# One attention kernel on one core: output bank and read banks take turns by head, new plan with 203 VectorE tiles

## The chip, the core and the metric

The kernel runs on one core of a Trainium2 chip. Five engines work side by side, each on its own queue of instructions in a fixed order: TensorE (PE in the profile, its weight loads PEld), VectorE (DVE), ScalarE (ACT), GpSimd (POOL) and SyncE (SP, which here only issues DMAs). They meet through semaphores: an instruction that has to wait holds up everything behind it on its own engine. TensorE writes its results into PSUM, which has 128 partitions and eight banks; a bank holds 512 float32 numbers for each partition. The metric is the time of one execution on the device in microseconds (us), lower is better. The median of runs is compared.

## The reference

```python
B, H, S, D = 1, 32, 2048, 640
Dh = D // H                       # 20
def reference(q, k, v, t):
    eps = 1e-6
    qn = q / (jnp.sqrt((q * q).sum(axis=-1, keepdims=True)) + eps)
    kn = k / (jnp.sqrt((k * k).sum(axis=-1, keepdims=True)) + eps)
    logits = jnp.einsum('bhqd,bhkd->bhqk', qn, kn) * t[None, :, None, None]
    attn = _softmax(logits, axis=-1)
    return jnp.einsum('bhqk,bhkd->bhqd', attn, v)
```

There are 32 heads of 2048 queries and 2048 keys with 20 features each, all in bfloat16. The logits are bounded (normalized rows times t), so no maximum is subtracted; the sum of the exponentials comes out of a column of ones beside v.

## The kernel before

**Tiles.** The keys of a head lie in 16 blocks of 128 (R = 16), its queries in 4 quarters of 512 (NG = 4). One block of keys against one quarter of queries is a unit: 128 x 512 logits, one PSUM bank. Four units that go into the same output matmuls are a tile, so a head has 16 tiles and the kernel 512. A tile is either ScalarE's or VectorE's. `DVE_TILES` (L715) gives VectorE's number for each head, 5 to 8; they sum to 206, so 306 tiles (1224 units) are ScalarE's.

**ScalarE's path.** TensorE multiplies units into `psA` (five banks, used as a set of two and a set of three; `add_wave`, L1142, matmul at L1073, tasks `q3A`). ScalarE takes the exponential of a whole set at once from `psA` into `p_ring` (L1165, tasks `exp`), so sets of 1024 and 1536 columns alternate. An `exp` can start when its set is multiplied, and the set can be multiplied again when its `exp` is done.

**VectorE's path.** TensorE multiplies two units' worth of packed logits at a time into the two banks of `psD` (L1078, tasks `q2D`, "the pair"). VectorE reads both banks in one instruction into `xt` (L1216, tasks `t1`): this builds bit patterns of an approximate exponential. Three shifted copies of it (tasks `s0`, `s1`, `s2`) are made by GpSimd (L1246, `ss`) or VectorE (L1236 into `ss`, L1234 into `sp`); the four versions are weighted and summed by the output matmuls. `xt` has 8 slots, `ss` and `sp` 4. The next pair waits for the `t1` that reads the same banks (`bank_t1`).

**Output.** Each group of four output matmuls (L1094, tasks `pv`) multiplies one version of a tile with v and adds into one bank, `psO`. A ScalarE tile has one group, a VectorE tile four. When all groups of head h are in, VectorE transposes the bank into `oT` (L1107, task `tr`, in `add_fin`, L1103), and later divides and stores, for two heads together (L1116, L1124). The first output matmul of head h+1 overwrites the bank, so `pv_base` (L1100) makes every `pv` of head h+1 wait for `tr` of head h.

**Other work.** VectorE also squares, sums and normalizes q and k of heads to come (L923 to L969); SyncE loads, transposes and rotates them. Groups of four matmuls with a zero weight (`pvnil`, L1004 to L1010) are put into idle stretches of TensorE and add zero to the open output bank.

**Order.** No queue is written out by hand. `list_schedule` (L151) plays the whole kernel through with a duration for each task and lets each engine take, whenever it is free, the best ready task by some twenty rules. The numbers in these rules (`KNOBS`, L103) are chosen anew for each 10 us of planned time; the choices are packed into the integers of `STAGES` (L108). The durations are constants in the code: a group on TensorE takes `PE_MM` = 0.223 us (L712), a change of its kind of matmul 0.097 us (L412, L581). The order found is emitted, with semaphore waits worked out by `plan_waits` (L626). The planned times themselves do not reach the chip, only the order of each queue.

PSUM before: `psA` five banks, `psD` two, `psO` one.

Of the kernel before, what the change touches and what calls it, by code (L numbers as in the profile page):

```python
# [54 lines left out]
class Task:  # L55
    __slots__ = ("eng", "fn", "dur", "deps", "pri", "name", "lat", "dma", "n", "users",
                 "start", "end", "seq", "inc", "cnt", "rows", "work", "modes", "win", "trig",
                 "alt", "parts", "parent", "rem", "glue", "room", "next", "head", "wide", "slow", "sdur", "pair", "base", "two", "need")

    def __init__(self, eng, name, fn, dur, deps, pri, lat=0.0, dma=None):  # L60
        self.eng, self.name, self.fn, self.dur = eng, name, fn, dur
        self.deps = [d for d in deps if d is not None]
        self.pri, self.lat, self.dma = pri, lat, dma
        self.inc, self.cnt = False, 0
        self.rows, self.work, self.modes = 128, 512.0, None
        self.win, self.trig = 0.0, None
        self.alt, self.parts, self.parent, self.rem = None, [], None, 0
        self.glue, self.room, self.next, self.head, self.wide = [], 0.0, None, None, None


        self.slow, self.sdur, self.pair, self.base, self.two = False, 0.0, None, dur, None

        self.need = None


Wake = Task("DVE", "wake", None, 0.0, [], 0.0)


class Program:
# [27 lines left out]
        "WAITH": (0.3, 0.1, 0.6), "BLOG": (5, 3, 4, 7, 9, 99), "PTWO": (1, 0), "STAY": (1, 0), "URGE": (3, 2, 4, 6), "BOOST": (1.0, 0.0, 0.4, 4.0), "DPV": (0.0, 0.3, 0.65, 1.0)}  # L107
    STAGES = (121198495550, 386731570679, 77123854022, 617480453033, 541694991365, 26516008980, 28188130953, 628587374903, 9557073731, 415555843896, 209498320437, 646470623202, 136583393724, 671941958076, 672324246996, 792421957682, 689380213680, 803027612629, 379997812126, 638643698950, 639121345246, 531136220444, 376259042864, 376617779119, 221897598895, 374543095684, 221362179218, 787313552789, 415913386058, 208446558798, 427204335065, 465723747116, 401404110210, 428458674786, 432937268058, 619977817991, 207993392811, 516782334303, 568560126277, 529856924852, 435260979089, 428752721390, 619855720106, 632747624100, 787539313032, 787849807561, 633115376521, 774950211778, 788266765840, 736861074358, 722791283681, 515990522269, 287562967953, 747408491084, 537279315194, 325670581757, 376196432267)  # L108

    def __init__(self):  # L110
        self.tasks = []
        self.nsw = 0
        self.filler, self.fillers = None, []
# [6 lines left out]
    def schedule(self):  # L120
        self.list_schedule()
        for f in self.tasks:
            if f.parts:
# [27 lines left out]
    def list_schedule(self, until=None):  # L151
        self.stage = None
        for t in self.tasks:
            t.users = []
            t.trig = None
            if t.modes:
                self.use(t, 0)
            if t.alt:
                t.eng, t.parts, t.slow, t.dur = "DVE", [], False, t.base
        for i, t in enumerate(self.tasks):  # L160
            t.seq = i
            deps = []
            for d in t.deps:
                deps += d() if callable(d) else [d]
            t.deps = list(dict.fromkeys(deps))
            t.n = len(t.deps)
            for d in t.deps:
                d.users.append(t)
# [223 lines left out]
        base, at_ = [0.0], {"e": 0, "t": 0}  # L392
        left = collections.Counter(t.head for t in self.tasks if t.head is not None)
# [3 lines left out]
        def fill(now):  # L397
# [10 lines left out]
            t = self.filler()  # L408
# [3 lines left out]
            if last_pe[0] != "pv":  # L412
                t.end += max(0.0, 0.097 - (now - free["PE"]))
# [8 lines left out]
        while events or ready["POOL"]:  # L422
# [20 lines left out]
            for e in touched:  # L443
# [7 lines left out]
                if e in soon:  # L451
                    wide = e == "PE" and self.QHOLD and any(
                        now < w <= now + self.QHOLD and self.tasks[q].name[2] == "A" for q, w in soon["PE"].items())
                    held = [r for r in ready[e] if wide and r[2].name[0] == "q" and r[2].name[2] == "D" or r[2].name[:2] not in ("t1", "tr") and
# [23 lines left out]
                elif e == "DVE" and self.CONT:  # L478
# [21 lines left out]
                    elif not sh:  # L500
                        x = min(ready[e])
                    else:
# [5 lines left out]
                        continue  # L508
                    ready[e].remove(x)
# [68 lines left out]
                if e == "PE":  # L578
                    kind = "pv" if t.rows > 128 else t.name[:2]
                    if kind != last_pe[0]:  # L580
                        t.end += max(0.0, 0.097 - (now - free["PE"]))  # L581
                        self.nsw += 1
# [3 lines left out]
                    recent.append((t.end, t.work))  # L586
                    if t.head is not None:
# [4 lines left out]
                if t.name[:3] in ("exp", "t1."):  # L592
                    at_[t.name[0]] += 1
                done += 1
# [25 lines left out]
            if self.CONT:  # L620
                done += cont_fill(now)
        self.order, self.free, self.ready = order, free, ready
# [59 lines left out]
def bass_standalone__qk_norm__prompt_kernel(  # L682
# [42 lines left out]
    with ExitStack() as es:  # L725
# [34 lines left out]
        psD = es.enter_context(nc.psum_tensor("psD", [128, 1024], F32))  # L760
        psO = es.enter_context(nc.psum_tensor("psO", [128, 512], F32))
# [237 lines left out]
        for i in range(NWARM):  # L999
            warm.append(add("PE", "warm", lambda e, tk: e.matmul(psO[:, :], ones[:, 0:128], ones[:, :], start=True, stop=True), PE_MM,  # L1000
# [3 lines left out]
        def null_mm(eng):  # L1004
            last = None
            for g in range(NG):
                last = eng.matmul(psO[32 * g:32 * g + 32, :], nil[:, :], ones[:, :], start=False, stop=False,  # L1007
                                  skip_group_check=True, tile_position=(0, 32 * g))
            return last
        prog.filler = lambda: Task("PE", "pvnil", lambda e, tk: null_mm(e), PE_MM, [z_nil, z_one], 0.0)  # L1010

        def first_head(rinv):
# [28 lines left out]
            for i in range(NWARM2):  # L1041
                warm.append(add("PE", "warm", lambda e, tk: e.matmul(psO[:, :], ones[:, 0:128], ones[:, :], start=True, stop=True), PE_MM, [tk_], -198))
# [46 lines left out]
        def pv_mm(eng, h, w_of, rhs_of):  # L1089
# [3 lines left out]
            for g in range(NG):  # L1093
                last = eng.matmul(psO[32 * g:32 * g + 32, :], w_of(g), rhs_of(g), start=start,  # L1094
# [4 lines left out]

        def pv_base(h):  # L1100
            return [ld_v[h]] + z_v[h % NV] + ([lambda: [trO[h - 1]]] if h else warm)

        def add_fin(h):  # L1103
# [4 lines left out]
                oT_all[:, so, :, :].rearrange("p r d -> p (r d)"), psO[:, :]), 0.63,  # L1108
# [33 lines left out]
        def add_wave(w):  # L1142
# [12 lines left out]
            qk = add("PE", f"q3A{w}", lambda e, tk: f_qk(e), PE_MM + 0.01, deps, w - 10000.0)  # L1155
# [37 lines left out]
        def add_dgroup(jg):  # L1193
# [9 lines left out]
            for bs in ((0,), (1,)) if SPLIT[j % len(SPLIT)] else ((0, 1),):  # L1203
                def f_qk(eng, bs=bs):
                    last = None
                    for b in bs:
                        last = qk_pair(eng, h, c, dl, b, psD[:, 512 * b:512 * b + 512])
# [7 lines left out]
                def read(name, dst, o, add_, deps, pri):  # L1215
                    return add("DVE", name, lambda e, tk: e.tensor_scalar(  # L1216
                        dst[:, o + 2 * w0:o + 2 * (w0 + n)].bitcast(I32), psD[:, w0:w0 + n], W_MUL, add_, ALU.mult, ALU.add),
# [132 lines left out]
```

## Time and profile before

| what | number |
|---|---|
| time, median of 3 runs | 577.32 us (576.85 to 577.65) |
| the profiled execution, its own time | 577.27 us |
| its span, first to last instruction | 575.5 us |
| granted TensorE clock, mean | 0.999 |
| busy PE, PEld | 554.6, 160.7 us |
| busy DVE, ACT, POOL | 556.9, 558.6, 453.0 us |
| transposes of the output bank (L1107) | 32, 715 ns each, 22.9 us together |
| reads of the pair (L1216) | 206, 1216 ns each, 250.4 us together |
| shifts by POOL (L1246) | 356, 443.8 us together |
| shifts by VectorE into sp (L1234), into ss (L1236) | 155, 188.7 us; 17, 11.1 us |
| zero groups (L1007) | 68 matmuls, 5.7 us |
| HBM traffic | 18 GB/s over the span |

In the lists of the profile a row names the line, the engine, the operation and `out<-in` by the program's names, then the count; busy time counts time in which at least one such instruction ran, so overlapping instructions (ScalarE's, TensorE's) have a mean that times the count exceeds it. "Idle before" is time the engine stood still just before such an instruction, and "<-" names what ended it. In a timeline a row is start, length, engine, line, and in brackets the idle time before it. The profiled execution lies 0.05 us from the median, and 1.8 us of its time lie outside of its span.

### The profile page before, as it was taken

The numbers are of one execution on the slowest core, as the hardware profiler recorded it, in microseconds if no ns is written. First come the engines' busy times: TensorE is split into PE (matmuls) and PEld (weight loads), VectorE is DVE, ScalarE is ACT, GpSimd is POOL, SyncE is SP. The second block draws the span as 40 slices with busy tenths as digits, with TensorE's granted clock in tenths as the row PEclk, the third lists the DMA queues.
The fourth block names the chain that finished last, engine by engine and source line by source line (L and its number), as shares of the span: only waits on it lengthen the run. The fifth ranks groups of instructions, "written<-read, shape, count | busy, mean of one in ns | idle before, by whom it ended". The sixth has DMA issues, their size and how long they took to land.

```text
span 575.5 us, 14801 instructions
## 1 busy us (share of the span) xinstructions
PE 554.6 (96%) x6255; PEld 160.7 (28%) x6255; DVE 556.9 (97%) x661; ACT 558.6 (97%) x497; POOL 453.0 (79%) x406
## 2 busy tenths in 40 slices
PE   7999999999999999999999999999999999999997
PEld 2222232222222222222222232222222222223333
DVE  8999999999999999999999999999999999999997
ACT  6999999999999999999999999999999999999992
POOL 6586985898598985997768795887949888688972
PEclk9999999999999999999999999999999999999999
DMA  5544513553354403653046420563205540241000
GB/s 67 65 75 84 61 16 70 88 90 31 67 85 52 76 1 72 88 64 57 2 95 75 76 35 11 100 79 69 22 21 101 72 75 2 50 80 40 2 2 18
DMA packets 190770, 32.18 MB, mean 56 GB/s; under 512 B 170608, under 2 KB 190704, under 8 KB 190704
## 3 DMA queue, kind: packets, MB, share of 16 engines
q1 hardware_dynamic: 190560, 31.15, 35.3%
q8 instruction: 49, 0.80, 0.6%
q14 instruction: 17, 0.14, 0.1%
q10 hardware_dynamic: 144, 0.08, 0.1%
HBM read 7.87 MB, written 2.62 MB: 18 GB/s over the span
## 4 chain that ended last, share of the span: by engine, by line
ACT 86%; PE 10%; POOL 1%; DVE 1%; issue 0%; POOLq 0%
ACT p_ring L1165 86%; PE psO L1094 7%; PE psA L1073 2%; PE psD L1078 1%; DVE oT L1107 0%; POOL p_ring L1053 0%; DVE ss L1236 0%; POOL pcol L829 0%; POOL vph L770 0%; DVE xt L1216 0%; POOL vaug L770 0%; DVE rs_sum L926 0%; POOL pcol L823 0%; PE psO L1007 0%; DVE o_stage L1124 0%
## 5 line engine op out<-in xcount | busy, mean ns | idle before, releaser
L1165 ACT ACTIVATE p_ring<-psA 128x1024 bf16<-128x1024 f32 x490 | 555.1, 1369 | 2.5 <-PE psA L1073 2.2
L1246 POOL INT64_ADD ss<-xt x356 | 443.8, 1265 | 114.5 <-PE psO L1094 40.9
L1216 DVE TENSOR_SCALAR xt<-psD 128x1024 int32<-128x1024 f32 x206 | 250.4, 1216 | 5.5 <-PE psD L1078 4.7
L1234 DVE TENSOR_SCALAR sp<-xt 128x1040 int32<-128x1040 int32 x155 | 188.7, 1225 | 0.5 <-PE psO L1094 0.3
L1073 PE MATMUL psA<-qkT,kR 32*128 32x512 bf16 x968 | 164.5, 384 | 8.9 <-ACT p_ring L1165 7.3
L1094 PE MATMUL psO<-ss,vph 128*32 128x512 bf16 (+1 forms) x1852 | 166.2, 393 | 0.8 <-DVE oT L1107 0.7
L1094 PE MATMUL psO<-p_ring,vaug 128*32 128x512 bf16 x1224 | 112.1, 383 | 0.4 <-DVE oT L1107 0.4
L1073 PEld LDWEIGHTS psA<-qkT,kR 32*128 32x128 bf16 x968 | 40.0, 91 | 154.3 <-ACT p_ring L1165 146.8
L1094 PE MATMUL psO<-xt,vaug 128*32 128x512 bf16 (+1 forms) x824 | 82.2, 394 | 0.6 <-DVE oT L1107 0.3
L1094 PE MATMUL psO<-sp,vph 128*32 128x512 bf16 (+1 forms) x620 | 65.1, 408 | 0.0
L1094 PEld LDWEIGHTS psO<-ss,vph 128*32 128x32 f16 x1852 | 43.8, 94 | 58.9 <-issue 34.0
L1078 PE MATMUL psD<-qP,kR 64*128 64x512 bf16 x284 | 55.4, 387 | 1.7 <-DVE xt L1216 1.5
L1073 PE MATMUL psA<-qkT 32*128 32x512 bf16 x256 | 53.6, 384 | 1.7 <-ACT p_ring L1165 1.3
L1094 PEld LDWEIGHTS psO<-p_ring,vaug 128*32 128x32 bf16 x1224 | 29.8, 94 | 40.0 <-issue 29.4
L1094 PEld LDWEIGHTS psO<-xt,vaug 128*32 128x32 bf16 x824 | 21.7, 94 | 28.8 <-issue 18.6
L1107 DVE STREAM_TRANSPOSE oT<-psO 128x512 f32<-128x512 f32 x32 | 22.9, 715 | 6.9 <-PE psO L1094 6.4
L1078 PE MATMUL psD<-qP,qkT 64*128 64x512 bf16 x128 | 24.9, 386 | 0.8 <-DVE qP L979 0.6
L1078 PEld LDWEIGHTS psD<-qP,kR 64*128 64x128 bf16 x284 | 13.6, 92 | 39.2 <-issue 22.8
L1073 PEld LDWEIGHTS psA<-qkT 32*128 32x128 bf16 x256 | 12.9, 90 | 40.8 <-ACT p_ring L1165 38.4
L926 DVE TENSOR_REDUCE rs_sum<-sq 128x64 f32<-128x1280 bf16 (+1 forms) x17 | 23.1, 1357 | 0.0
L969 DVE TENSOR_TENSOR qkn<-qk_sb,rs_r 128x1280 bf16<-128x1280 bf16 (+1 forms) x17 | 22.9, 1367 | 0.0
L1094 PEld LDWEIGHTS psO<-sp,vph 128*32 128x32 f16 x620 | 16.3, 94 | 21.2 <-issue 10.4
(66 smaller groups left out, 129.1 us busy)
## 6 DMA issues: line engine op xcount, KB each, us to landing
kR<-qkT SPq DMA_DIRECT2D x62, 96.0 KB, 2.2
kR<-qkT SPq DMA_DIRECT2D x62, 64.0 KB, 2.1
qk_sb<-in_k_dram SPq DMA_DIRECT2D x32, 80.0 KB, 3.1
vaug<-in_v_dram SPq DMA_DIRECT2D x32, 80.0 KB, 3.3
qk_sb<-in_q_dram SPq DMA_DIRECT2D x124, 20.0 KB, 2.5
out_dram<-o_stage SPq DMA_DIRECT2D x31, 80.0 KB, 1.8
kR<-qkT SPq DMA_DIRECT2D x62, 32.0 KB, 1.9
qkT<-qkn SPq DMA_TRANSPOSE x31, 3.2
```

The lines of the kernel that those rows point to most:

```text
L926: sums.append(dv("sum", lambda e, tk, i=i, m2=m2, src=src: e.tensor_reduce(rs["sum"][:, 2 * R * i:2 * R * i + m2], src, AXIS_X, ALU.add), ...
L969: norm[h] = [dv("norm", lambda e, tk, x=x, b=b, i=i, m=m: e.tensor_tensor(qkn_all[:, b:b + m, :, :].rearrange("p n r w -> p (n r) w")[:, : ...
L1073: return eng.matmul(dst, k_of(h, c, (rho - g) % 4, ps), qkT[h % NT][ps, 0:512], tile_position=(32 * g, 0))
L1078: return eng.matmul(dst, k_of(h, c, dl, ps), qP[h % NT][ps, :], tile_position=(64 * b, 0))
L1094: last = eng.matmul(psO[32 * g:32 * g + 32, :], w_of(g), rhs_of(g), start=start, stop=False, skip_group_check=True, tile_position=(0, 32 * g))
L1107: trO[h] = add("DVE", f"tr{h}", lambda e, tk: e.transpose(oT_all[:, so, :, :].rearrange("p r d -> p (r d)"), psO[:, :]), 0.63, [lambda: pv ...
L1165: act[w] = add("ACT", f"exp{w}", lambda e, tk: e.activation(p_ring[:, p0 * 512:p0 * 512 + n], psA[:, slot * WAVES[0] * 512:slot * WAVES[0] ...
L1216: return add("DVE", name, lambda e, tk: e.tensor_scalar(dst[:, o + 2 * w0:o + 2 * (w0 + n)].bitcast(I32), psD[:, w0:w0 + n], W_MUL, add_, ...
L1234: return e.tensor_scalar(sp[:, oe, :, :].bitcast(I32)[:, :, 0:PAD], xt[0][:, bx:bx + TILE].bitcast(I32), float(PHASE_W[i]), None, ALU.add)
L1246: f.alt = lambda c, n, i=i, dst=dst: lambda e, tk: e.int64_add(dst[:, be + 2 * c:be + 2 * (c + n)].bitcast(I64), xt[0][:, bx + 2 * c:bx + ...
```

## The change

Three things change together.

**Banks.** `psD` and `psO` become one tensor `psF` of three banks. The output of an even head goes into its first bank, that of an odd head into its third. The pair uses the other two: the second and third while an even head is open, the first and second while an odd one is. So head h+1 accumulates into a bank that the pair has used until then, and the pair moves onto the bank that head h has used.

**Waits and plan.** A pseudo task `bank{h}` stands in `pv_base` where the transpose of the head before stood. In the plan it is set free by a function `flip`, when no more than `FLIP` (0, 2 or 4) groups of the open head are left, no pair stands unread, and the transpose of the head before that is out; on the chip it becomes two waits, for the last `t1` issued before it and for `tr{h-1}` of the head that used the bank two heads ago. From then on each new pair waits for `tr` of the head just closed (`t.deps.append(self.trO[self.given - 1])`), and the planner does not issue a pair until that transpose is planned to be over (`shut`). Two knobs, `FLIP` and `FSOON`, are new. The zero groups go to the bank of the open head.

**Numbers.** `PE_MM` goes from 0.223 to 0.226, the cost of a change of kind from 0.097 to 0.102, a set's own price from `PE_MM + 0.01` to `PE_MM + 0.005`. `DVE_TILES` of the last three heads goes from 6, 7, 8 to 7, 6, 5, all others stay, so 203 tiles are VectorE's and 309 (1236 units) ScalarE's. `STAGES` is new from the first entry to the last, so the order of every queue may differ everywhere.

```diff
@@ class Program: KNOBS
-        "WAITH": (0.3, 0.1, 0.6), "BLOG": (5, 3, 4, 7, 9, 99), "PTWO": (1, 0), "STAY": (1, 0), "URGE": (3, 2, 4, 6), "BOOST": (1.0, 0.0, 0.4, 4.0), "DPV": (0.0, 0.3, 0.65, 1.0)}
+        "WAITH": (0.3, 0.1, 0.6), "BLOG": (5, 3, 4, 7, 9, 99), "PTWO": (1, 0), "STAY": (1, 0), "URGE": (3, 2, 4, 6), "BOOST": (1.0, 0.0, 0.4, 4.0), "DPV": (0.0, 0.3, 0.65, 1.0), "FLIP": (0, 2, 4), "FSOON": (0.3, 0.0, 0.8)}
...
@@ list_schedule: leave
+            t.left = True
...
-                    lat += self.TR_SLACK if t.name[:2] == "tr" else self.PV_SLACK
+                    lat += self.TR_SLACK if t.name[:2] in ("tr", "ba") else self.PV_SLACK
...
+        self.given, asked, read, self.pair_of = 0, [0], [0], {}
+        last_t1, due_ = [None], [False]
+
+        def flip(now):
+
+            h = self.given
+            if due_[0]:
+                if asked[0] > read[0]:
+                    return
+                due_[0], h = False, h - 1
+            else:
+                if h + 1 not in self.bank_of or left[h] > self.FLIP or (
+                        asked[0] > read[0] and left[h]) or h and not self.trO[h - 1].left:
+                    return
+                if left[h] and any(not u.left and (u.n or rt[u.seq] > now + self.FSOON) for u in self.pv_users[h]):
+                    return
+                self.given = h + 1
+                if asked[0] > read[0]:
+                    due_[0] = True
+                    return
+            f = self.bank_of[h + 1]
+            f.parts = [x for x in (last_t1[0], self.trO.get(h - 1)) if x]
+            f.end = max([x.end for x in f.parts] + [0.0])
+            leave(f, now)
+
+        def shut(now):
+
+            h = self.given
+            return h and not (self.trO[h - 1].left and self.trO[h - 1].end + self.SEM_LAT["DVE"] + self.TR_SLACK <= now + 1e-9)
...
-                t.end += max(0.0, 0.097 - (now - free["PE"]))
+                t.end += max(0.0, 0.102 - (now - free["PE"]))
...
-                    held = [r for r in ready[e] if wide and r[2].name[0] == "q" and r[2].name[2] == "D" or r[2].name[:2] not in ("t1", "tr") and
+                    no = e == "PE" and shut(now)
+                    held = [r for r in ready[e] if no and r[2].name[:3] == "q2D" or wide and r[2].name[0] == "q" and r[2].name[2] == "D" or r[2].name[:2] not in ("t1", "tr") and
...
+                    if t.name[:3] == "q2D":
+                        asked[0] += 1
+                        self.pair_of[int(t.name[3:].split(".")[0])] = 512 * (1 - self.given % 2)
+                        if self.given:
+                            t.deps.append(self.trO[self.given - 1])
...
@@ the kernel
-    PE_MM = 0.223
+    PE_MM = 0.226
...
-    DVE_TILES = [5, 6, 6, 6, 7, 6, 7, 6, 7, 6, 7, 6, 7, 6, 7, 6, 6, 7, 6, 7, 6, 7, 6, 7, 6, 7, 6, 7, 6, 6, 7, 8]
+    DVE_TILES = [5, 6, 6, 6, 7, 6, 7, 6, 7, 6, 7, 6, 7, 6, 7, 6, 6, 7, 6, 7, 6, 7, 6, 7, 6, 7, 6, 7, 6, 7, 6, 5]
...
-        psD = es.enter_context(nc.psum_tensor("psD", [128, 1024], F32))
-        psO = es.enter_context(nc.psum_tensor("psO", [128, 512], F32))
+
+        psF = es.enter_context(nc.psum_tensor("psF", [128, 3 * 512], F32))
+        psO = [psF[:, 0:512], psF[:, 1024:1536]]
+        psD = psF[:, 512:1536]
...
-                last = eng.matmul(psO[32 * g:32 * g + 32, :], w_of(g), rhs_of(g), start=start,
+                last = eng.matmul(psO[h % 2][32 * g:32 * g + 32, :], w_of(g), rhs_of(g), start=start,
...
+        bank_of = {h: Task("DVE", f"bank{h}", None, 0.0, [], 0.0) for h in range(1, H)}
...
-            return [ld_v[h]] + z_v[h % NV] + ([lambda: [trO[h - 1]]] if h else warm)
+            return [ld_v[h]] + z_v[h % NV] + ([bank_of[h]] if h else warm)
...
-                oT_all[:, so, :, :].rearrange("p r d -> p (r d)"), psO[:, :]), 0.63,
+                oT_all[:, so, :, :].rearrange("p r d -> p (r d)"), psO[h % 2]), 0.63,
...
-            qk = add("PE", f"q3A{w}", lambda e, tk: f_qk(e), PE_MM + 0.01, deps, w - 10000.0)
+            qk = add("PE", f"q3A{w}", lambda e, tk: f_qk(e), PE_MM + 0.005, deps, w - 10000.0)
...
-                        last = qk_pair(eng, h, c, dl, b, psD[:, 512 * b:512 * b + 512])
+                        last = qk_pair(eng, h, c, dl, b, psF[:, prog.pair_of[j] + 512 * b:prog.pair_of[j] + 512 * b + 512])
...
-                        dst[:, o + 2 * w0:o + 2 * (w0 + n)].bitcast(I32), psD[:, w0:w0 + n], W_MUL, add_, ALU.mult, ALU.add),
+                        dst[:, o + 2 * w0:o + 2 * (w0 + n)].bitcast(I32), psF[:, prog.pair_of[j] + w0:prog.pair_of[j] + w0 + n], W_MUL, add_, ALU.mult, ALU.add),
```

More of the change, by code (lines that the diff above doesn't have):

```diff
@@ L57 @@
                  "start", "end", "seq", "inc", "cnt", "rows", "work", "modes", "win", "trig",
-                 "alt", "parts", "parent", "rem", "glue", "room", "next", "head", "wide", "slow", "sdur", "pair", "base", "two", "need")
+                 "alt", "parts", "parent", "rem", "glue", "room", "next", "head", "wide", "slow", "sdur", "pair", "base", "two", "need",
+                 "own", "left")
     def __init__(self, eng, name, fn, dur, deps, pri, lat=0.0, dma=None):
@@ L421, in list_schedule @@
         recent = collections.deque()
-        while events or ready["POOL"]:
+        forced = [False]
+        while events or ready["POOL"] or ready["DVE"]:
+            if not events and ready["DVE"]:
+                forced[0] = True
+                base.append(0)
+                events.append((max(free.values()), 2, -1.0 * len(base), Wake))
             if not events and self.CONT:
@@ L593, in list_schedule @@
                     at_[t.name[0]] += 1
+                if t.name[:3] == "t1.":
+                    read[0] += 1
+                    last_t1[0] = t
+                elif t.name[:2] == "tr" and t is self.trO.get(self.given - 1):
+                    base.append(0)
+                    heapq.heappush(events, (t.end + self.SEM_LAT["DVE"] + self.TR_SLACK, 2, -1.0 * len(base), WakePE))
                 done += 1
```

43 lines of the change are left out of this document (26 added, 17 removed).

## The prediction

> **What bounds the kernel now.** I read the busy shares first: PE 96%, DVE 97%, ACT 97% of the span. Shares so close say nothing, so the chain of waits came next; by engine it reads
>
> ```profile
> ACT 86%; PE 10%; POOL 1%; DVE 1%; issue 0%; POOLq 0%
> ```
>
> so ScalarE's queue of exponentials sets the end. The table by stretch of time shows how tightly (columns: stretch and length, then busy us of PE, PEld, DVE, ACT, POOL, then clock, DMA share, GB/s):
>
> ```profile
> 300.00:400.00 100.00, 98.14 (x1116) 27.63 (x1116) 98.35 (x110) 100.00 (x89) 82.75 (x58) 1.00 0.44 65
> 400.00:500.00 100.00, 98.55 (x1105) 27.00 (x1103) 97.75 (x113) 99.89 (x89) 80.35 (x59) 1.00 0.28 44
> 564.98:575.50 10.52, 6.95 (x124) 4.28 (x116) 7.59 (x11) 0.01 (x1) 2.93 (x4) 0.94 0.08 25
> ```
>
> ACT is never free in the middle, DVE is some 2% free, and there is a last stretch of 10.5 us without ScalarE. "Never free" hides something: successive exponentials overlap in the record. An unhindered run of them is in the timeline, the whole in the chain in order of time:
>
> ```profile
> 101.66 10.49 ACT L1165 ACTIVATE p_ring<-psA 128x1536 bf16<-128x1536 f32 x9 [1.01 <-PE psA L1073]
> ```
>
> ```profile
> 101.66 338.96 ACT p_ring L1165 x299
> ```
>
> Nine that begin and end with a wide one (1581 ns) give (10.49 - 1.58) / 4 = 2.228 us for a narrow and a wide set; the long stretch gives 338.96 / 149.5 = 2.267. The difference, 0.039 x 245 pairs = 9.6 us over the kernel, is ScalarE waiting a few hundredths at a time for its logits. That is the most that a better order in the middle can return to ScalarE at an unchanged split of tiles.
>
> The waits show what a change of head costs (engine and line, whom it waited for, us in total, times, longest):
>
> ```profile
> PEld psO L1094 <- DVE oT L1107: 7.1, 20, 0.6
> DVE oT L1107 <- PE psO L1094: 6.4, 17, 0.8
> DVE xt L1216 <- PE psD L1078: 4.7, 13, 1.1
> ```
>
> and a timeline of one change shows its form:
>
> ```profile
> 458.16 0.41 PE L1094 MATMUL psO<-sp,vph 128*32 128x512 bf16 x4
> 458.51 0.39 PE L1078 MATMUL psD<-qP,qkT 64*128 64x512 bf16 x2
> 458.63 0.72 DVE L1107 STREAM_TRANSPOSE oT<-psO 128x512 f32<-128x512 f32 x1 [0.53 <-PE psO L1094]
> ...
> 459.27 1.18 DVE L1216 TENSOR_SCALAR xt<-psD 128x1024 int32<-128x1024 f32 x1
> 459.40 0.10 PEld L1094 LDWEIGHTS psO<-xt,vaug 128*32 128x32 bf16 x4 [0.40 <-DVE oT L1107]
> ```
>
> The last output group ends, the transpose follows, the next head's output starts 0.05 us after it. What matters here is the second row: the pair is multiplied *before* the transpose, so VectorE goes from the transpose straight into a read. Going through the 31 inner transposes in VectorE's timeline I count 25 that a read of the pair follows at once.
>
> **The change, part by part.** The sum is made against the profiled execution (577.27 us, 0.05 below the median; span 575.5).
>
> *Three tiles fewer for VectorE: 12 units more for ScalarE.* L1165 is busy 555.1 us for 1224 units, 0.4535 us each, so 12 cost 5.44 us (2.228 / 5 x 12 = 5.35 unhindered: both ends lie together). They lie on the path: the last exponential moves from 564.98 to 570.4. TensorE gets three output groups and five sets more, 12 groups and three pairs fewer; nothing of that is on the path.
>
> *The tail.* It reads today
>
> ```profile
> 549.44 15.54 ACT L1165 ACTIVATE p_ring<-psA 128x1024 bf16<-128x1024 f32 x14
> 568.14 1.89 DVE L1236 TENSOR_SCALAR ss<-xt 128x1024 int32<-128x1024 int32 x3
> 571.29 0.65 PE L1094 MATMUL psO<-p_ring,vaug 128*32 128x512 bf16 x8
> 571.97 0.72 DVE L1107 STREAM_TRANSPOSE oT<-psO 128x512 f32<-128x512 f32 x1 [0.82 <-PE psO L1094]
> 573.01 0.49 DVE L1124 TENSOR_TENSOR o_stage<-oT,rec 128x320 bf16<-128x320 f32 x1
> ```
>
> ScalarE ends at 564.98, but VectorE still shifts versions of the last head's eight tiles until 570.03, and 8.3 us of output groups (35) follow the last set of logits. The last head now has five tiles. A tile costs VectorE 250.4 / 206 + (188.7 + 11.1) / 206 = 2.19 us, so three save 6.6 us and its shifts end near 563.5, before ScalarE. What must follow the last exponential is then a group and the transpose (0.65 + about 0.2 for the waits) and 575.5 - 571.97 = 3.5 us to the end: 4.3 us at least. At most it is today's 10.5 us less nine groups (12 of three tiles fewer, three of ScalarE's more) at 8.3 us for 35 groups: 10.5 - 9 x 0.24 = 8.4. I take 5.0, since VectorE's part falls away. Together with the 5.44 us: 570.4 + 5.0 = 575.4, against 575.5. **The new split is worth -0.1 us**, between -0.8 and +3.3.
>
> *Waits that go.* TensorE's 7.1 us at L1094 behind the transpose go, since the new head's bank is free once the last read is done. That is off the path in itself; it gives TensorE room to deliver logits on time. VectorE's 6.4 us before transposes have less reason, since no output waits any more, and a shift can be put in front. But the pair now waits for the same transpose, which needs the last group as before. I let half fall: -3.2 us, between 0 and -6.4.
>
> *Waits that come.* No pair can be multiplied between the bank's hand-over and the end of the transpose. From a pair to its read takes 0.43 us where VectorE stood waiting:
>
> ```profile
> 557.26 0.39 PE L1078 MATMUL psD<-qP,kR 64*128 64x512 bf16 x2
> 557.69 1.23 DVE L1216 TENSOR_SCALAR xt<-psD 128x1024 int32<-128x1024 f32 x1 [0.26 <-PE psD L1078]
> ```
>
> with the 0.05 us to TensorE that is 0.48 us in which VectorE has no read. Cover is a shift of 1.23 us (L1234); where one is ready the cost is nothing, and where none is, 0.48 us. For the 25 places the ends are 0 and 12.0 us. The nearest row is the one that exists for reads that waited for their pair: 4.7 us in 13 waits, 0.36 each; for two thirds of 25 places, since a shift isn't always at hand with four slots and GpSimd taking most of them, that is 25 x 2/3 x 0.36 = 6.0 us. Behind the held pair stand, in TensorE's queue, the next sets for ScalarE and the output groups; once a pair is late on the chip, ScalarE's logits are late too, beyond the one set that it has in hand (0.9 to 1.3 us).
>
> *Costed at nothing:* the zero groups in another bank, the DMAs, whose number and sizes stay (HBM at 18 GB/s; no wait of ScalarE or VectorE for a DMA over 0.7 us in the list, all in the first 4 us or 0.2 us long; if that cover goes, a late load stops VectorE's squares, which are wanted heads later), the durations in the planner (they only choose the order).
>
> **Sum.** -0.1 - 3.2 + 6.0 = +2.7 us, which VectorE can't hide: to head 30 its share is the same 6 to 7 tiles a head and it is free only 2%. 577.3 + 2.7 = **580.0 us**. In the middle, an order "planned anew" can also return up to 9.6 us or lose as many; that is in the cases below.
>
> The Trainium skill, "Perfetto Trace Analysis", Matmuls, says that independent matmul groups should rotate through different PSUM banks, so that the reading out of one overlaps the next group's matmuls. The 7.1 us row bears it out for the output; by the same rule the pair, which loses its own bank during the transpose, gets worse. By its first half alone the sum would be that of the faster case below, by both halves that of the forecast.
>
> **The rivals.**
> *Faster: TensorE's freedom is what ScalarE lacked.* Place: sets of logits that come hundredths late. The planner now uses durations a little longer than before, so its order slips less against the chip, and 7.1 us of TensorE's waits are gone. If half of the 9.6 us returns and shifts cover every transpose: 577.3 - 0.1 - 4.8 = 572.4. For it: the waits are real and sit at each head. Against: of TensorE's waits few end in ScalarE's (2.2 us shown in all, two thirds of it before 17 us and the rest at 101). Chance 0.28.
> *The same: the wait changes place only.* What leaves L1107 appears at L1216: 577.3 - 0.1 = 577.2. This includes that the bank is handed over so late (last read, and nearly all groups of the old head in) that the new head's output starts no earlier. Chance 0.16.
> *Much slower: no cover anywhere.* 25 x 0.48 = 12.0 us, none of the 6.4 returned: 589. It decides from the point where shifts in front of the next read run out. Chance 0.12.
> *The forecast*, 578.5 to 584: chance 0.44.
>
> **How the numbers follow.** About 0.2% (1.15 us) is what a measurement of this kernel can tell from no change. Slower 0.44 + 0.12 = 0.56, same 0.16, faster 0.28. The likeliest case gives 580. For 8 in 10 the range reaches into the faster case, whose lower half (all 9.6 us back would be 567.6) is left out, and up to the fully uncovered one: 572 to 588. The forecast's own range is 578.5 to 584.
>
> **What would show it.** Right: waits of L1216 (in its new place) for the pair grow from 4.7 towards 10 us, with the transpose as what the pair's weight load waits for; waits of output groups for the transpose all but vanish; after a transpose VectorE shifts or stands still before it reads; the last exponential ends past 570 and the tail is near 5 us. Wrong: if the pace of the exponentials comes down from 2.267 towards 2.228 us a pair, the faster case holds; if the tail stays above 8 us, the split was mis-sized; if reads wait no more than now and the time grows all the same, the cause is the new order and not the bank.

## The result, and the profile after

| | before | after |
|---|---|---|
| time, median | 577.18 us (576.85 to 577.65, 6 runs) | 579.42 us (579.02 to 579.83, 6 runs) |
| ratio | | 1.0038, 95% interval 1.0025 to 1.0051 |
| span of the profiled execution | 575.5 us | 577.3 us |
| end of the last exponential | 564.98 us | 571.75 us |
| from there to the end | 10.55 us | 5.53 us |

The change costs 2.2 us. The profiled execution after took 579.02 us, the shortest of its six, so the traces show 1.8 us of it. The chain of waits of the kernel after, by engine, hardly differs, and the table by stretch (stretch and length, busy us of PE, PEld, DVE, ACT, POOL, clock, DMA share, GB/s) shows ScalarE never free in the middle:

```profile
ACT 84%; PE 10%; DVE 2%; POOL 1%; DMA 1%; issue 0%; SPq 0%; POOLq 0%
```

```profile
300.00:400.00 100.00, 98.40 (x1102) 28.09 (x1094) 97.90 (x109) 100.00 (x90) 81.98 (x65) 1.00 0.43 62
400.00:500.00 100.00, 98.52 (x1110) 27.50 (x1114) 98.58 (x112) 100.00 (x89) 82.31 (x72) 1.00 0.29 46
564.98:577.30 12.32, 8.71 (x118) 2.86 (x115) 8.39 (x10) 6.78 (x7) 5.16 (x5) 1.00 0.07 21
```

The last row begins where ScalarE had ended before: now it works on for 6.78 us. The new thing is in the chain in order of time (start, length, what; consecutive exponentials are one piece):

```profile
26.08 67.00 ACT p_ring L1228 x59
...
98.04 1.04 PE psF L1154 x13
99.36 0.60 SPq L827
100.01 3.14 DMA kR<-qkT
103.64 396.96 ACT p_ring L1228 x351
```

Between two long runs of exponentials stands a gap in which the chain goes over SyncE and a load of rotated keys (`kR`); before, the chain entered its long run of exponentials at 101.66 with 1.01 us of idle time. The waits at a change of head (engine, line, whom it waited for, us, times, longest):

```profile
DVE xt L1279 <- PE psF L1138: 6.9, 18, 0.9
...
DVE oT L1170 <- PE psF L1154: 5.6, 12, 1.7
...
ACT p_ring L1228 <- PE psA L1133: 4.5, 5, 2.9
...
PEld psF L1138 <- DVE oT L1170: 0.9, 2, 0.5
```

The output groups' 7.1 us behind the transpose have fallen to 0.2; reads wait for their pair for 6.9 us instead of 4.7, transposes for the last group 5.6 instead of 6.4, and the pair's weight load waits for the transpose only twice. The timeline of one change of head shows why:

```profile
461.17 1.22 DVE L1279 TENSOR_SCALAR xt<-psF 128x1024 int32<-128x1024 f32 x1
...
462.30 0.71 DVE L1170 STREAM_TRANSPOSE oT<-psF 128x512 f32<-128x512 f32 x1
462.54 0.10 PEld L1154 LDWEIGHTS psF<-ss,vph 128*32 128x32 f16 x4 [0.23 <-DVE xt L1279]
...
462.93 1.20 DVE L1297 TENSOR_SCALAR sp<-xt 128x1040 int32<-128x1040 int32 x1
```

The next head's output starts *while* the old head's bank is being transposed, and after the transpose VectorE shifts. Counted over VectorE's timeline, a read follows the transpose at once in 25 of the inner changes before and in none after: 20 times it is a shift into `sp`, else a reciprocal, a square sum, a normalization or the like. The cover that the prediction doubted is always there: the planner holds a pair back until the transpose is over (`shut`), and VectorE's queue has other work in that place.

Nor do the longer waits of the reads stand at the changes of head. Of the 18 waits, four come within 3 us of the start of a transpose, 1.0 us together (before: one, 0.2 us); the others come 4 us or more behind it, or before the first transpose.

**Where the 1.8 us of span came from.** ScalarE's time from start to start, set by set, less what unhindered sets take in this trace (1.3305 us for a wide one, 0.904 for a narrow one) is its lateness. Last exponential: 12 units at 5.36 us unhindered, and lateness grown from 9.7 to 11.1 us, +1.4; tail 5.0 us shorter; 5.4 + 1.4 - 5.0 = 1.8. Lateness by stretch:

| us | before | after |
|---|---|---|
| start to 99 | 2.1 | 2.1 |
| 99 to 106 | 1.27 | 3.31 |
| 106 to 200 | 1.14 | 0.80 |
| 200 to 300 | 0.99 | 1.15 |
| 300 to 400 | 1.95 | 1.13 |
| 400 to 500 | 1.39 | 1.10 |
| 500 to 530 | 0.52 | 1.14 |
| later | 0.34 | 0.34 |

One stall adds 2.0 us; everywhere else together the new order is 0.7 us better. What leads to the stall is work for a head to come. First VectorE and SyncE before, then after (timelines; squares, their sum, the transposing DMAs, the rotations):

```profile
81.66 1.09 DVE L923 TENSOR_TENSOR sq<-qk_sb 128x1280 bf16<-128x1280 bf16 x1
...
83.86 1.48 DVE L926 TENSOR_REDUCE rs_sum<-sq 128x64 f32<-128x1280 bf16 x1
...
92.93 2.66 SPq L987 DMA_TRANSPOSE qkT<-qkn  x2
...
96.74 4.50 SPq L767 DMA_DIRECT2D kR<-qkT  x6
```

```profile
86.36 1.25 DVE L983 TENSOR_TENSOR sq<-qk_sb 128x1280 bf16<-128x1280 bf16 x1
...
88.67 0.70 DVE L1170 STREAM_TRANSPOSE oT<-psF 128x512 f32<-128x512 f32 x1
89.30 1.44 DVE L986 TENSOR_REDUCE rs_sum<-sq 128x64 f32<-128x1280 bf16 x1
...
94.22 5.10 SPq L1047 DMA_TRANSPOSE qkT<-qkn  x3
...
99.36 4.91 SPq L827 DMA_DIRECT2D kR<-qkT  x7
```

Squares come 4.7 us later, a third transposing DMA stands in SyncE's queue ahead of the rotations, and these start 2.6 us later. From 81 to 100.5 us no wait for a bank of `psF` is longer than 0.23 us. But order and banks are not fully apart here: the square sum that comes late stands right behind a transpose (88.67), in the place of the read that followed there before, so it is itself one of the covers. Whether the planner would have had the squares late without the new wait is not shown.

### The profile page after: what moved, and what is told of

The parts are those of the page before. It is cut to its first block, busy times and chain, and to the rows that moved or that the text cites. A ratio compares the mean times of both kernels' runs of the same rounds, so it can differ in the third digit from the quotient of the medians.

```text
span 577.3 us, 14766 instructions
## 1 busy us (share of the span) xinstructions
PE 558.6 (97%) x6225; PEld 156.4 (27%) x6225; DVE 556.7 (96%) x657; ACT 563.2 (98%) x502; POOL 450.6 (78%) x435
## 4 chain that ended last, share of the span: by engine, by line
ACT 84%; PE 10%; DVE 2%; POOL 1%; DMA 1%; issue 0%; SPq 0%; POOLq 0%
ACT p_ring L1228 84%; PE psF L1154 6%; PE psA L1133 3%; PE psF L1138 1%; DMA qkT<-qkn 1%; DVE xt L1279 1%; DMA kR<-qkT 1%; DVE ss L1299 1%; POOL p_ring L1113 0%; POOL pcol L889 0%; POOL vph L830 0%; POOL vaug L830 0%; DVE qkn L1029 0%; DVE oT L1170 0%; DVE rs_sum L986 0%
## 5 line engine op out<-in xcount | busy, mean ns | idle before, releaser
L1279 DVE TENSOR_SCALAR xt<-psF 128x1024 int32<-128x1024 f32 x203 | 247.0, 1217 | 8.0 <-PE psF L1138 6.9
L1154 PE MATMUL psF<-ss,vph 128*32 128x512 f16 (+1 forms) x1800 | 162.9, 394 | 0.0
L1154 PE MATMUL psF<-p_ring,vaug 128*32 128x512 bf16 x1236 | 115.4, 384 | 0.0
L1154 PE MATMUL psF<-xt,vaug 128*32 128x512 bf16 (+1 forms) x812 | 81.7, 394 | 0.3 <-DVE xt L1279 0.3
L1154 PE MATMUL psF<-sp,vph 128*32 128x512 bf16 (+1 forms) x636 | 66.7, 409 | 0.0
L1154 PEld LDWEIGHTS psF<-ss,vph 128*32 128x32 f16 x1800 | 42.3, 94 | 54.6 <-issue 34.0
L1138 PE MATMUL psF<-qP,kR 64*128 64x512 bf16 x278 | 54.2, 387 | 0.7 <-DVE xt L1279 0.7
L1154 PEld LDWEIGHTS psF<-p_ring,vaug 128*32 128x32 bf16 x1236 | 30.5, 94 | 42.2 <-issue 34.2
L1170 DVE STREAM_TRANSPOSE oT<-psF 128x512 f32<-128x512 f32 x32 | 22.8, 712 | 6.0 <-PE psF L1154 5.6
L1138 PE MATMUL psF<-qP,qkT 64*128 64x512 bf16 x128 | 24.9, 386 | 1.1 <-DVE qP L1039 0.8
```

The costliest lines, as they stand in the source:

```text
L1138: return eng.matmul(dst, k_of(h, c, dl, ps), qP[h % NT][ps, :], tile_position=(64 * b, 0))
L1154: last = eng.matmul(psO[h % 2][32 * g:32 * g + 32, :], w_of(g), rhs_of(g), start=start, stop=False, skip_group_check=True, tile_position=( ...
L1170: trO[h] = add("DVE", f"tr{h}", lambda e, tk: e.transpose(oT_all[:, so, :, :].rearrange("p r d -> p (r d)"), psO[h % 2]), 0.63, [lambda: p ...
L1279: return add("DVE", name, lambda e, tk: e.tensor_scalar(dst[:, o + 2 * w0:o + 2 * (w0 + n)].bitcast(I32), psF[:, prog.pair_of[j] + w0:prog ...
```

## The experiments

The theory to test: *banks and split are worth nothing, the loss is the order around the stall*. The rival: *the banks cost, through the pair that waits for the transpose and the read that waits for the pair*. In the edits `behind(engine, task, i, other, j)` moves one task of a planned queue to stand right behind another on that engine; waits are then worked out from the new order. Ratios are to the kernel before in the same comparison.

| run | median us | ratio, 95% interval |
|---|---|---|
| e1_sp_order | 579.13 | 1.0032, 1.0019 to 1.0045 |
| e2_sp_tr | 579.06 | 1.0029, 1.0019 to 1.0039 |
| e3_output_waits_again | 601.01 | 1.0414, 1.0398 to 1.043 |
| e4_pair_waits | 587.41 | 1.0169, 1.0155 to 1.0183 |
| e5_sets_earlier | 578.56 | 1.0023, 1.0012 to 1.0034 |
| e6_before_sets_earlier | 577.10 | 0.9993, 0.9985 to 1.0002 |
| e7_split_alone | 577.35 | 1.0000, 0.9991 to 1.0009 |
| e8_split_back | 587.18 | 1.0171, 1.0153 to 1.019 |
| e9_resequenced | 579.79 | 1.0044, 1.0031 to 1.0058 |
| e10_before_resequenced | 578.28 | 1.0018, 1.0009 to 1.0027 |
| e11_whole_queue | 621.37 | 1.0758, 1.0744 to 1.0773 |
| e12_whole_queue_old_banks | 611.03 | 1.0583, 1.0559 to 1.0607 |

**The stall, by SyncE's and VectorE's queues.** e1 in the changed kernel, and e2 with both lines:

```diff
         prog.schedule()
+        behind("SP", "trn7", 0, "rot5", -1)
+        behind("DVE", "tr3", 0, "norm5", -1)
         prog.plan_waits()
```

> The changed kernel; in SyncE's queue alone the transpose of head 7 goes behind the six rotations of head 5. Everything else keeps its order. Theory A (most of the loss is one stall of ScalarE, 2.87 us at 100.8 us, because the rotations of head 5 were issued at 99.4, 5.1 us after the transposes began, instead of some 3.8 us): the stall shrinks by 1.3 us to about 1.5 us, and since ScalarE has no slack behind it, the time falls by the same, 579.4 to about 578.1. Theory B (the pairs that wait for transposes, 31 times, are the loss): the time stays within 0.4 us of 579.4, what is saved here is lost at the next head changes.

> As e1, and in VectorE's queue the transpose of head 3 goes behind the two normalizations of heads 5 to 8, so that these come 0.7 us earlier. Theory A: the stall is 2.87 - 1.3 - 0.7, about 0.9 us, and the time about 577.4, level with the kernel before. Theory B: within 0.4 us of 579.4.

In e1 the rotations came 2 us earlier (97.30 instead of 99.36) and the stall shrank from 2.87 to 2.46 us. The medians, 0.3 and 0.4 us below the changed kernel's, lie where the rival expected them, and their intervals overlap its interval. In e2's timeline:

```profile
95.59 4.90 ACT L1228 ACTIVATE p_ring<-psA 128x1536 bf16<-128x1536 f32 x4
...
102.97 4.62 ACT L1228 ACTIVATE p_ring<-psA 128x1536 bf16<-128x1536 f32 x4 [2.48 <-PE psA L1133]
```

The keys were there now, but TensorE, which takes its queue in order, first had eight output groups to do that stood between the pair and the next set. The late DMA was one of two things that end there together. In e2 what was gained stayed: ScalarE's sets ran 0.27 us earlier than in the changed kernel ahead of the stall and 0.67 us earlier from there to the end, and so did reads and transposes from 157 us on. In e1 they ran 0.26 us earlier ahead of it, 0.66 us at 121 us, but only 0.15 us from 175 us on: the gain was lost again behind the stall.

**The two banks' waits, each laid on an order not made for it.** e3 lets every output group of head h+1 that stands behind the last one of h wait for the transpose again, in the changed kernel. e4 lets, in the kernel before, the first pair behind the last output group of a head (if its read is after the transpose) wait for that transpose:

```diff
+        for i, u in enumerate(pe):                # e3
+            if u.head and i > last[u.head - 1]:
+                u.deps.append(trO[u.head - 1])
...
+                if u.name[:3] == "q2D" and read[u.name[3:].split(".")[0]] > dv.index(trO[h]):   # e4
+                    u.deps.append(trO[h])
+                    break
```

> The changed kernel in its own order; the output groups of head h+1 that stand behind the last group of head h wait for the transpose of head h again, as before the change. Theory A (the early hand-over of the bank is used by this order, and TensorE has no room left to make it up): each of 30 changes costs some 0.3 us or more of TensorE's time, 8 to 12 us in all, time 587 to 591. Theory C (the early hand-over frees TensorE only where nobody waited for it): less than 1 us, 579.4 to 580.4.

> The kernel before in its own order and banks; the first pair behind the last output group of a head that is read after the transpose waits for that transpose (31 pairs), which is the wait that the change adds, without an order made for it. The prediction's price: 0.36 to 0.48 us at the 25 places where a read follows the transpose at once, 9 to 12 us, time 586 to 589. Rival: VectorE's free 2% and ScalarE's set in hand swallow it: 0 to 3 us, 577 to 580.

e3 costs 21.6 us against the changed kernel, about twice what was expected, and e4 10.2 against the kernel before, as expected. Waits of e3, then of e4, and a change of head in e4:

```profile
PEld psF L1154 <- DVE oT L1170: 33.4, 30, 2.5
...
DVE xt L1279 <- PE psF L1138: 27.9, 40, 4.2
...
ACT p_ring L1228 <- PE psA L1133: 21.0, 29, 3.4
```

```profile
PEld psD L1078 <- DVE oT L1107: 24.9, 27, 1.7
...
DVE xt L1216 <- PE psD L1078: 16.0, 37, 0.7
```

```profile
448.99 0.72 DVE L1107 STREAM_TRANSPOSE oT<-psO 128x512 f32<-128x512 f32 x1
...
449.76 0.39 PE L1078 MATMUL psD<-qP,qkT 64*128 64x512 bf16 x2 [0.49 <-DVE oT L1107]
...
450.19 1.23 DVE L1216 TENSOR_SCALAR xt<-psD 128x1024 int32<-128x1024 f32 x1 [0.49 <-PE psD L1078]
```

So both waits are real and dear where the order does not provide for them. The reads of e4 wait 16.0 us instead of 4.7, and its time grows by nearly as much: at 22 of the 25 places where a read follows the transpose VectorE stands 0.49 us, at one 0.71 us. The changed kernel escapes that price (6.9 us) by its order, and that order rests on the early hand-over: with it taken away it loses 21.6 us. A part of both losses goes with TensorE at half clock, which the last section comes back to.

**The sets in TensorE's queue.** Following e2, e5 moves a pair and two sets of that stretch ahead; e6 makes the like moves in the kernel before:

```diff
+        behind("PE", "q2D30.0", 0, "pv0.27", 0)
+        behind("PE", "q3A82", 0, "pv2.27", 0)
+        behind("PE", "q3A81", 0, "pv2.27", 0)
```

> e2 with one more edit: in TensorE's queue the first pair and the two sets of logits of head 5 go in front of the output groups that filled the planned wait (nine groups, 2.2 us). In e1 and e2 the rotations landed some 1.3 us earlier, but TensorE ran those groups back to back up to 102.5 us, so the stall only fell from 2.87 to 2.5 us and the time by 0.3 us. Theory A (the stall near 101 us is passed on to the end in full): the stall falls to 0.3 to 0.7 us, the time by 1.8 to 2.2 us against e2, to 576.9 to 577.3. Theory B (the pairs' new wait is the loss and later head changes take back what is saved): 578.7 to 579.4.

> The kernel before with the same kind of edit in TensorE's queue: first pair and two sets of head 5 in front of five output groups. Its stall at 101 us is 1.01 us. If such a stall passes to the end in full, the time falls by 0.7 to 1.0 us, 577.25 to 576.2 to 576.5, and the changed kernel without its stall (e5) is some 0.7 us slower than this one; if not, 577.2.

In e5 the stall is split in two, since the groups pushed back now stand ahead of the set after:

```profile
101.52 2.37 ACT L1228 ACTIVATE p_ring<-psA 128x1536 bf16<-128x1536 f32 x2 [0.66 <-PE psA L1133]
...
105.37 2.37 ACT L1228 ACTIVATE p_ring<-psA 128x1536 bf16<-128x1536 f32 x2 [1.49 <-PE psA L1133]
```

Another 0.5 us came back: 578.56, 0.9 us below the changed kernel by the three edits together. Six of e5's seven runs lie below every run of the changed kernel, though the two intervals overlap; between the two traces the gain behind the stall is 0.5 us. Both theories had expected another time. In e6 the stall falls only from 1.01 to 0.47 us, and the kernel before gains nothing that can be told (577.10).

**The split by itself.** e7 is the kernel before with the new `DVE_TILES`, e8 the changed kernel with the old:

```diff
-    DVE_TILES = [..., 6, 7, 8]
+    DVE_TILES = [..., 7, 6, 5]
```

> The kernel before with 7, 6, 5 tiles for VectorE in the last three heads and nothing else; its order is the same to 527 us. The sum of the two traces (12 units more, +5.4 us; the tail 5.0 us shorter) gives +0.4 us: 577.7, with ScalarE ending near 570.4 and a tail near 5.5 us. If the split itself were the loss, it would be 579 or more; if it gained as the prediction's lower end, 576.4.

> The changed kernel with 6, 7, 8 tiles in the last three heads as before; its order is the same to 527 us. The knobs of its last stretches were chosen for 7, 6, 5. If 203 tiles suit the turning banks in themselves, ScalarE ends 5.4 us earlier, near 566.3, and the tail grows by more than it, to 12 us or more: 580 to 585. If the split is as good as neutral, as the prediction had it: 579 to 580.

e7 ends its last exponential at 571.29 and its span 4.75 us later: 576.05 against 575.5, the median 577.35, ratio 1.0000. The split is worth nothing. But e7 is also the fairer partner for the changed kernel, as it has the same tiles, and its tail is 0.8 us shorter (4.75 against 5.53 us). The chain in order of time, e7 and then the changed kernel, shows where: behind the last set of logits TensorE has output groups for 0.7 us more.

```profile
569.89 2.56 PE psO L1094 x44
```

```profile
570.43 3.28 PE psF L1154 x51
```

e5, measured beside e7, is 1.2 us slower by the medians; of that the two traces show 0.8 us in the tail and 0.2 us in lateness (10.55 against 10.38). So what e5 leaves of the loss is mostly in the tail, and no run here tests what makes that longer.

In the changed kernel the new split can't be taken back: e8 (587.18) is slower than either expectation, presumably because the planner's rules for the end were chosen with it. What is left after the last exponential in e8 is

```profile
566.56:585.74 19.18, 12.58 (x174) 4.22 (x166) 15.21 (x16) 0.00 (x0) 10.29 (x10) 1.00 0.05 14
```

19.2 us, in which VectorE (15.2 us busy) reads and shifts the last tiles one after the other. That run speaks of its own end and says nothing on the banks.

**A stretch of TensorE's queue merged anew.** e9 takes e2, moves the first pair of that stretch ahead and merges sets 81 to 112 with the other work, so that each set comes as soon as ScalarE has freed its banks; e10 does the same to e7, on the old banks.

> e2 with TensorE's queue merged anew between set 81 (the first of head 5, 101 us) and set 112: each set of logits goes to where its bank pair should be free, all other groups keep their order among themselves. In e5 the stall of 2.5 us came back as two, 1.1 us at 101.5 and 1.6 us at 105.4, because the groups that had been pushed back stood in front of the next set. If TensorE has the room to work these groups off over 35 us, the lateness of ScalarE's sets between 99 and 106 us falls from 2.7 to about 1.0 us, and the time by the same against e5, 578.6 to 576.9, half a microsecond under the kernel before: then the turning banks cost nothing in themselves and the loss was the order around head 5. If TensorE's backlog is the bound there, lateness only spreads over the next windows and the time stays at 578.2 to 578.8.

> The kernel before with 7, 6, 5 tiles in the last three heads (e7) and the same merging of TensorE's queue between sets 81 and 112, the first pair of head 5 five groups earlier. Its lateness between 99 and 106 us is 1.27 us. With room on TensorE: 0.5 us, time 577.35 to 576.6, the best of all; without: 577.2 or more.

The stall is gone in e9, lateness between 99 and 106 us falls to 0.95, but between 106 and 200 us it rises from 0.80 to 4.03. In e9's timeline:

```profile
123.50 0.72 DVE L1170 STREAM_TRANSPOSE oT<-psF 128x512 f32<-128x512 f32 x1 [0.69 <-PE psF L1154]
124.27 0.10 PEld L1138 LDWEIGHTS psF<-qP,kR 64*128 64x128 bf16 x2 [1.34 <-DVE oT L1170]
...
125.36 4.62 ACT L1228 ACTIVATE p_ring<-psA 128x1536 bf16<-128x1536 f32 x4 [0.91 <-PE psA L1133]
```

Here is the forecast's mechanism in full: the pair waits for the transpose, the set behind it in TensorE's queue comes late, ScalarE stands. With ScalarE 2 us ahead and VectorE not, the cover made for the old timing no longer fits. It costs 0.7 us over e2. But the same merging costs 0.9 us over e7 on the old banks, where no pair waits for a transpose (lateness between 106 and 200 us rises there from 1.14 to 2.35), so such a merging fails with either banks. Neither gave the gain that was hoped for.

**The whole queue.** To see if a better TensorE order favours either set of banks, e11 (on e2) and e12 (on e7) have over half of its 1862 tasks in new places (1005 and 965 moved against the rest), in a fixed order written into the kernel; the other queues stay.

> The changed kernel with the two moves of the second experiment (SyncE's seventh transposing DMA behind the last rotation of the fifth block, VectorE's third transposed sum behind the fifth's scaling), and TensorE's queue reworked over its whole length: sets, pairs and output groups change places with their neighbours from the sixth set to the last; all other queues stay. Theory one: the three banks are worth nothing either way and the whole loss is the order. Then a rework of the whole queue takes back at least the 2.0 us that ScalarE loses at 99 to 106 us and some of its remaining 9 us of lateness: 576 to 577.2 us, and no more than 0.5 us above the next kernel, which has the old banks and the same kind of rework. Theory two: the banks themselves cost, by VectorE's reads, which wait for their pairs 2.2 us longer than before: the kernel stays 1.2 us or more above the next one. Theory three, from the resequenced kernel (579.79 us): what TensorE gives ScalarE early, VectorE's reads take back, and the time stays at 579 us or above.

> The kernel before with the new split of VectorE's tiles (203) and its old banks, and TensorE's queue reworked over its whole length in the same way as in the kernel beside it. If rework pays at all, it comes below 577.35 us, the time of this kernel without it: 575.5 to 577. Theory one expects it within 0.5 us of the kernel with the turning banks; theory two expects it 1.2 us or more below; theory three expects no gain here either, 577.3 us or above, as with the resequenced stretch (578.28 us).

No theory foresaw a loss of this kind: the gains expected of a better order missed by 30 us and more, and that e11 ends 10.3 us above e12 can't be counted for the theory that the banks cost. e11's waits:

```profile
PEld psF L1138 <- DVE xt L1279: 49.0, 82, 3.8
...
ACT p_ring L1228 <- PE psA L1133: 41.4, 43, 4.1
...
PE psF L1138 <- DVE xt L1279: 24.1, 26, 3.5
```

In the changed kernel the last of these is 0.9 us in 3 waits. A queue drawn so tight has TensorE at the pair before VectorE has read the last one; each slip stops the sets behind it, and a stop of TensorE costs its clock on top (last section). e12 (611.03) has the same in a milder form. The pair of runs says nothing on the banks: whether they would be ahead under an equally good order stays open.

## Why the prediction was right, point by point

The time (579.42 for 580.0), the sign and the range were right. The mechanism that was to give the sign was not: reads left without cover at the changes of head do not occur after the change, and the 2.2 us come from elsewhere. Of the signs named, four came true (output groups no longer wait for the transpose, VectorE shifts behind it, the last exponential ends at 571.75, the tail is 5.5 us); the one that stood for the mechanism, the pair's weight load waiting for the transpose, came 0.9 us in 2 waits.

- *The split, -0.1 us*: right. e7 measures 0.0, with a tail of 4.75 us for the 5.0 taken. In the changed kernel the tail is 5.53.
- *Waits that come, +6.0 us*: mis-sized. Reads waited for their pair 2.2 us more in all, 0.8 of it within 3 us of a transpose. "For two thirds of 25 places" was the failing step: the order puts other work of VectorE behind every inner transpose, so no read stands there without cover. The price of an uncovered place was sound: 0.49 us in e4 for the 0.48 forecast, and e4, with 31 such waits under the old order, pays 10.2 us against 12.0 forecast for no cover at all, in part with the clock.
- *Waits that go, -3.2 us*: mis-sized. Transposes waited only 0.8 us less; at the 31 changes of head it is 1.7 (5.6 to 3.9), while the last wait, in the tail, grew from 0.8 to 1.7. TensorE's 7.1 us did go, and are off the path, as was said; but e3 shows that they cannot be had back for 7.1, since a whole order now rests on the early hand-over.
- The two terms together were to give +2.8 and gave +1.4 (2.2 - 0.8) of VectorE's time. It would be wrong to book this as the loss. What ScalarE lost is 1.4 us net, 2.0 of it in the one stall between 99 and 106 us, where late squares and a third transposing DMA hold the rotated keys and eight output groups stand ahead of the next set. The prediction named that ("a late load stops VectorE's squares, which are wanted heads later" and "lose as many" by a new plan) but gave it no term. That the size came out close is luck: two terms that did not occur as forecast add up to nearly what a stall, a gain elsewhere and a longer tail happened to leave.
- *The faster rival*: its place was right, its size was not. From 106 to 530 us lateness fell from 6.0 to 5.3 us, 0.7 and not 4.8. The 9.6 us behind it was ScalarE's lateness in the whole kernel (9.7 set by set), of which 3.4 lies ahead of 106 us and was not there to be had in the middle. And of ScalarE's 2.2 us of shown waits, 1.2 lie before 17 us, a little over half and not two thirds.
- *The test "if reads wait no more than now and the time grows all the same, the cause is the new order"* gives a mixed answer: they wait more, mostly away from the changes of head. e1, e2 and e5 shift tasks alone, banks untouched, and by the medians take 0.9 of the 2.2 us back. The other 1.3 us could not be recovered by moving single tasks; 0.8 us of it is the longer tail by the traces. That it is the order's too is not shown, nor is what the order would be without the new wait, since the only plan with these banks was made with it.

## What to carry to other kernels

Rotating a bank away from one user takes it from another; here the price was paid only where the engine in between had nothing else to do (e4), so count what follows each hand-over in the *new* order and not in the old. In this kernel of coupled in-order queues, what e2 and e5 saved at one local stall reached the end undiminished (0.4 and 0.5 us), while e9, which cleared the stall on one engine, met a new wait on another. Look for such stalls in start-to-start times of the bounding engine: its busy time reads 99.9 to 100 us of each 100 in both kernels.

## What the runs showed of the hardware

TensorE's clock fell to half for windows of 3.41 us (or two in a row) in the runs where it had to stand. e11, then e4, in stretches that end at such windows' edges (the column before the DMA share is the clock):

```profile
75.48:78.89 3.41, 2.30 (x25) 0.69 (x21) 3.41 (x4) 3.37 (x4) 2.63 (x3) 1.00 0.50 85
78.89:82.30 3.41, 3.41 (x27) 0.71 (x23) 3.11 (x3) 2.40 (x3) 0.31 (x1) 0.50 0.21 16
82.30:85.71 3.41, 3.41 (x44) 1.03 (x46) 3.06 (x3) 2.73 (x3) 2.32 (x2) 1.00 0.00 0
```

```profile
103.08:106.49 3.41, 2.09 (x25) 0.54 (x21) 3.29 (x4) 3.41 (x4) 3.34 (x4) 1.00 0.40 108
106.49:109.90 3.41, 3.41 (x21) 0.68 (x21) 2.37 (x2) 2.38 (x3) 2.90 (x4) 0.50 0.79 110
```

TensorE was idle for 1.11 and 1.32 us of the 3.41 us ahead, in pieces of at most 0.9 and 1.1 us, and ScalarE then lost about 1 us in the slow window. Taken over all fourteen kernels, on the grid of these windows and between a kernel's first and last sets: no window at full clock with less than 1.1 us idle was followed by half clock, every one with over 1.65 us was, and in between both occur. The most that the changed kernel has between its first and last sets is 0.9 us, so it stays at 1.00. e11 has ten half-clock windows between, 34 us at half speed, up to 17 us of TensorE's work out of the 42 us that it lost against e2; e12, on the old banks, has ten too; e3 has two and e4 one, up to 3.4 and 1.7 us of their 21.6 and 10.2. Of e4's four runs one kept the full clock (1.000 against 0.996 and 0.997): it took 585.72 us and the others 587.35 to 587.50, so the lower clock went with some 1.7 us. The Trainium skill, "TensorE: Matmul & The Clock Gate", Part 1, gives a free-running window of 3413 ns and has the clock fall after at least one idle window. The length agrees with the 3.41 us here. The condition, read as a window without work, does not: a window idle for one third was enough.
